# RWKV-7 recurrence and a hard-swish feed-forward on one core: parametric Relus in the weight conversion, and four edits of order

## The chip, the core and the metric

The kernel runs on one core of one Trainium2 chip. Its time is the device time of one execution in microseconds (us), and less is better. Of the kernel before there are three timed runs; beside them one execution was taken by the hardware profiler. The engines are called as in the profile: PE is TensorE's matmul and PEld its weight load, DVE is VectorE, ACT is ScalarE, POOL is GpSimd, SP is SyncE, which here only issues DMAs. L312 is line 312 of the kernel before.

## What is computed

The inputs r, k, v, w, a, b are float32 of 4 batches x 8 heads x 768 positions x 40 features. For each batch and head a 40x40 state runs along the positions:

```python
y[t]  = r[t] @ state
Sa    = state @ a[t]
state = state * w[t] - outer(Sa, b[t]) + outer(v[t], k[t])
```

The outputs y, 3072 tokens of 8 x 40 = 320 features, go through a feed-forward block:

```python
h = x @ w_in                    # 320 -> 2048
g = h * clip(h + 3, 0, 6) / 6
out = g @ w_out                 # 2048 -> 320
```

The two weights come as float64. The kernel sees each element as two 32-bit words (raw[..., 0] the low one, raw[..., 1], called hi, the high one with the sign, 11 bits of exponent and 20 of mantissa) and makes float32 of them itself.

## The kernel before

**The recurrence** is computed in blocks of 64 positions (BL). A unit i is one such block of two batches with all 8 heads; there are 24 units, and four of them (NU) make a group. `prepare(i)` holds the stages that need no state: W (turn w on PE, copy it into wm by L480 and L481 on ACT, one scan on DVE, L484), gam (reciprocal L495, small copies on POOL, the fetch of V), A, B and K (turn the input, multiply by the scan's products; rgam L510, at L513, bt L521, kt L603), factor (rgt on ACT, KBt L590 on POOL), F, E (scores and their mask, L467), EV. `invert` (L643) inverts the lower triangles of a whole group: `fb` and `x` are made first, then 60 dependent small DVE operations (L660 and L666), then two transposes (tb, tt). `third_block` (L685) completes each inverse by two matmul steps, with copies to zs and tinv on ACT; for the first group (`first`) it copies in two halves (`parts`, L689), and POOL copies the diagonal blocks (L710, L711). `step(i)` holds what needs the state: RT, VT, R, S, U (copy L814), UT, C, rS, sn, H, y, and move, which brings the result into xt.

**The feed-forward stream** is a generator whose pieces are put between the other work by `pieces(n)`. A job is one unit and one half of the 2048 features: `expand` issues 32 wide matmuls and a narrow part (`short`: the third 64 rows of the features), whose end leads to L989 (Relu of h + 3 on ACT) and L990 (min and product on DVE); `contract` issues the second matmul (L1015), one job later. While `spread[0]` is set, `short` is not issued at the end of `expand` but later, at the latest after the sixth matmul of the next `contract` (LATEST). h has two PSUM banks, which one job fills. The last jobs are drained by L1334 and L1335.

**The weights** are read in 20 pieces of 128 partitions x 512 elements (`load_weights`, L255). Each call of `next(weights)` takes one step of the conversion:

- L299 (DVE, shift and mask, exponent) and L301 (ACT, Relu with the bias `low`),
- L307 (DVE, low word to the mantissa of the piece before),
- L312 (DVE, product, the piece before is done; a new piece may be loaded),
- L320 (DVE, sign to the exponent),
- L325 (DVE, mantissa bits) and L328 (ACT, to a number in [1, 2)).

So there are five steps to a piece. They are handed out by counters: `fill` and MIXED in the first group's preparation, every third turn of the loop at L1133 while the first inversion runs, and 1.5 or 3 of them for each matmul stage of PLAN (L1161), the written-out order of the first group's `step` stages. In `run` the steps come between a stage's matmuls and the copies of its results. The first feed-forward jobs need 10 pieces, the others all 20.

**Order.** Every engine executes its own instructions in the order of the program, and that order is written out by hand. `by_twos` (L1093) prepares the first and the second group: at t = 0 the stage W of units 0 and 1, at t = 1 gam of both, then A; at t = 3 the stages W of units 2 and 3 and then B of units 0 and 1. All loads go through SP's queue but those of W for unit 1 and one of R, which ACT issues. After the second group `a_block`, `together` and `feed` put the remaining units in between the feed-forward pieces.

Of the kernel before, what the change touches and what calls it, by code (L numbers as in the profile page):

```python
# [8 lines left out]
F32 = mybir.dt.float32  # L9
I32 = mybir.dt.int32  # L10
# [8 lines left out]
HB = BL // 2  # L19
L = 32  # L20
SLOT = 64


def _ap(ap, extra, dims):
# [5 lines left out]
def kernel(  # L30
# [113 lines left out]
    nc.vector.memset(three[:], 3.0)  # L144
    warm = const.tile([P, 1], F32, name="warm")
    nc.scalar.activation(out=warm[:], in_=three[:], func=AF.Relu)
    low = const.tile([P, 1], F32, name="low")
    nc.vector.memset(low[:], -896.0 * 2 ** 23)


    AHEAD = NU + 1
# [103 lines left out]
    def load_weights():  # L255

        todo, homes = weight_pieces(), raw_homes()
        loaded, done, issued = deque(), [], [0]
        upcoming = []

        def load():
            if issued[0] == min(PIECES, limit[0]):
                return False
            if not upcoming:
                upcoming.append(next(homes))
            raw, before = upcoming[0]  # L270
            if before is not None and before not in done:
                return False
            upcoming.clear()
            issued[0] += 1
            out, loads = next(todo)
            for to, src in loads(raw):
                nc.sync.dma_start(out=to, in_=src)
            loaded.append((out, raw))
            return True

        while load():
            pass
        refill.append(load)
        phase[0] = 0
        yield
        before = None
        parts = [grp.tile([P, HD + WPAD], F32, name=f"parts{n}", tag="KBt", bufs=NU + 2)
                 for n in range(2)]
        parts = [t[:, 0:2 * WC].bitcast(U32).rearrange("p (n c) -> p n c", n=2) for t in parts]
        for n in range(PIECES + 1):  # L290
            now = None
            if n < PIECES:
                while load():
                    pass
                out, raw = loaded.popleft()
                hi = raw[:, :, :, 1]
                x = parts[n % 2]
                now = out, raw, x
                nc.vector.tensor_scalar(x, hi, 20, 0x7FF, ALU.logical_shift_right,  # L299
                                        ALU.bitwise_and)  # L300
                nc.scalar.activation(out=x, in_=x, func=AF.Relu, bias=low[:], scale=2.0 ** 23)  # L301
                phase[0] = 1
                yield
            if before:
                out, raw, y = before
                m, yf = raw[:, :, :, 1].bitcast(F32), y.bitcast(F32)
                nc.vector.scalar_tensor_tensor(m, raw[:, :, :, 0], 2.0 ** -52, m, ALU.mult, ALU.add)  # L307
                phase[0] = 2
                yield
                if len(out.shape) == 4:  # L310
                    m, yf = (z.rearrange("p n (j c) -> p n j c", c=out.shape[3]) for z in (m, yf))
                nc.vector.tensor_tensor(out=out, in0=m, in1=yf, op=ALU.mult)  # L312
                converted[0] += 1
                done.append(n - 1)
                while load():
                    pass
                phase[0] = 3
                yield
            if now:
                nc.vector.scalar_tensor_tensor(x, hi, 0x80000000, x, ALU.bitwise_and,  # L320
                                               ALU.bitwise_or)
                phase[0] = 4
                yield

                nc.vector.tensor_scalar(hi, hi, 0xFFFFF, 0x4B000000, ALU.bitwise_and,  # L325
                                        ALU.bitwise_or)
                m = hi.bitcast(F32)
                nc.scalar.activation(out=m, in_=m, func=AF.Copy, bias=-7.0, scale=2.0 ** -20)  # L328
                phase[0] = 5
                yield  # L330
            before = now

    def weight_pieces():

# [51 lines left out]
    def fetch(name, i, engine=None):  # L386

        if i is None or i >= NK:
            return
        x, crossed = {"W": (w, 0), "A": (a, 0), "B": (b, 0), "K": (k, 0), "R": (r, 1),  # L390
                      "V": (v, 1)}[name]
        if name == "V":
            t = values[i % AHEAD]
        else:
            t = (others if i < 2 * NU and i % 2 and name != "R" else inputs)[name]
        g, p = names[i]
        engine = engine or nc.sync
        for q in range(2):
            y = x[2 * p + q, :, g * BL:(g + 1) * BL, :]
            rows = slice(q * BL, (q + 1) * BL)  # L400
            if crossed:
                for s in range(2):
                    engine.dma_start(out=t[rows, 4 * s:4 * s + 4, 0:D],
                                     in_=y[s::2].rearrange("h t e -> t h e"))
            else:
                engine.dma_start(out=t[rows, :, 0:D], in_=y.rearrange("h t e -> t h e"))
        data[i][name + "N"] = t
# [63 lines left out]
    def prepare(i, F):  # L471
        n, o = i % NU, data[i]
        halves = i >= 2 * NU
        def w_stage():
            wt = turn_pairs(o["WN"])
            yield PE

            wv = wm[:].rearrange("p (r m i) -> p r m i", m=2, i=HB + 1)
            x = wt[:].rearrange("p r (q m i) -> p (r q) m i", q=2, m=2)
            nc.scalar.activation(out=wv[:, :, 0, 1:HB + 1], in_=x[:, :, 0, ::-1], func=AF.Copy)  # L480
            nc.scalar.activation(out=wv[:, :, 1, 1:HB + 1], in_=x[:, :, 1, :], func=AF.Copy)  # L481
            fetch("W", following(i))
            prods = o["prods"] = tmp.tile([P, NB, 2, HB + 1], F32, name="prods", bufs=2)
            nc.vector.tensor_tensor_scan(  # L484
                out=prods[:].rearrange("p r m i -> p (r m i)"), data0=wm[:], data1=start[:],
                initial=0.0, op0=ALU.mult, op1=ALU.add,
            )
# [197 lines left out]
    def third_block(F, tb, tt, n, first=False):  # L685


        zs = tmp.tile([P, 2, H, L], F32, name="zs")
        parts = [slice(0, H // 2), slice(H // 2, H)] if first else [slice(0, H)]  # L689
        zp = ps_pair(H, L)  # L690
        for h in range(H):
            for y in range(2):
# [314 lines left out]
    def contract(i, r, gts):  # L1007
# [13 lines left out]
        if r == 0:  # L1021
            sums[i] = op
            if split:
                part = ffn.tile([P, 3 * P], F32, name="part", tag="xt", bufs=6)[:, 0:DM]
                nc.scalar.activation(out=part, in_=op[:], func=AF.Copy, scale=1.0 / 6.0)
                sums[i] = part
        else:
            ob = ffn.tile([P, DM], F32, name="ob", bufs=OB)
            if split:
                nc.vector.scalar_tensor_tensor(out=ob[:], in0=op[:], scalar=1.0 / 6.0,  # L1030
                                               in1=sums.pop(i), op0=ALU.mult, op1=ALU.add)
            else:
                nc.scalar.activation(out=ob[:], in_=op[:], func=AF.Copy, scale=1.0 / 6.0)
            del ready[i]
            g, p = names[i]
            for q in range(2):
                row = (2 * p + q) * T + g * BL
                nc.sync.dma_start(out=out[row:row + BL, :], in_=ob[half(q)])
        yield True


# [45 lines left out]

    STAGES = 9

    RFETCH, EARLY, MIXED = 8, 5, 1 / 3  # L1090
    TWOS = 14

    def by_twos(first, steps, mixed, rate, fill={}):  # L1093


        chains = [by_stages(first + i, prepared(first + i)) for i in range(NU)]
        for t in range(TWOS):

            order = [0, 1] if t < STAGES else []
            order += [2, 3] if t > 5 else []  # L1100
            if t == 3:
                order = [2, 3, 0, 1]
            for i in order:
                run(chains[i], steps if t > 10 else 0, fill.get(t, 0), mixed)
                pieces(rate / 2)
            if t == 10:
                side.append(invert(group_F[-1], third, first == 0))
            yield
# [2 lines left out]
    ring.clear()  # L1111
    ring.extend([("any", 5)] * 5 + [("h", 2)] * 2)
    for name in "WABK":
        for i, engine in enumerate((nc.sync, nc.scalar if name == "W" else nc.sync)):
            fetch(name, i, engine)
    for t, _ in enumerate(by_twos(0, 4, MIXED, 0, {5: 1, 6: 1, 10: 1})):
        if t == 0:
            next(weights)
        limit[0] = {7: 4, 10: 12}.get(t, limit[0])
# [13 lines left out]
    while not third:  # L1133
        aside(1)
        if not third:
            n += 1
            if n % 3 == 1:
                next(weights, None)
            if converted[0] == 2 and not cleared:
                cleared.append(nc.gpsimd.memset(tinv[:], 0.0))  # L1140
            if n % EARLY == 0 and early:
                run(early.popleft())
    assert not early and cleared
    limit[0] = 13
    while phase[0] in (1, 2, 3):
        next(weights)
    firsts = [third_block(*third[-1], n, True) for n in (0, 2)]
    run(firsts[0])
# [181 lines left out]
    for _ in range(2):  # L1330
        for _ in a_block(m):
            pass
        m += 1
    while jobs or next(stream):  # L1334
        next(stream)  # L1335

# [29 lines left out]
```

## Time and profile before

| | |
|---|---|
| median of 3 runs (lowest, highest) | 831.4 us (829.04, 831.72) |
| the profiled execution | 831.98 us, its span 830.2 us |
| PE busy in the span | 746.4 us |
| DVE busy in the span | 547.4 us |
| ACT busy in the span | 321.7 us |
| POOL busy in the span | 156.1 us |
| mean granted TensorE clock | 0.938 |

The span begins with the first instruction and ends with the last; 1.78 us of the execution lie around it. A line of the timeline gives start, duration, engine, line, operation, output and input, and in brackets how long the engine was idle before it and what ended that. Durations of neighbouring DVE and ACT instructions overlap by some 0.1 us, so that sums of durations are a little above the time taken.

### The profile page before, as it was taken

To read this page: it belongs to the slowest core of one execution; us is meant where nothing else is said; L and a number is where in the kernel's file an instruction comes from. 1 tells how busy PE (TensorE), PEld (TensorE's weight loads), DVE (VectorE), ACT (ScalarE), POOL (GpSimd) and SP (SyncE) were. 2 spreads that over 40 slices of the span, in tenths; PEclk is the share of its full clock that TensorE was granted. 3 is DMA by queue.
4 is the path that set the end of the run, shared out by engine and by line. 5 is a ranking of instruction groups with operands and counts; after the bars stand their busy time and mean duration, and the time that the engine had idled before them with its cause. 6 is when DMAs were issued, how large, how long until landed. Compare 5 with 4: busy or idle time off the path is not lost.

```text
span 830.2 us, 35843 instructions
## 1 busy us (share of the span) xinstructions
PE 746.4 (90%) x15832; PEld 632.0 (76%) x15832; DVE 547.4 (66%) x1108; ACT 321.7 (39%) x864; POOL 156.1 (19%) x305
## 2 busy tenths in 40 slices
PE   4732877898999999999999999999999999999997
PEld 3622766686887878788888888878888888888875
DVE  7999697988964769844589654799556685232201
ACT  1323744232344533454433635334553334322211
POOL 3231301122112230321220222112212102000000
PEclk7755587999999999999999999999999999999999
DMA  7573344331133230322331332232232101100000
GB/s 141 85 187 85 91 113 100 70 62 25 21 59 65 52 66 19 59 46 48 56 51 28 60 62 44 42 58 36 45 60 48 22 20 29 29 20 16 15 18 16
DMA packets 174218, 45.05 MB, mean 54 GB/s; under 512 B 157424, under 2 KB 172784, under 8 KB 174064
## 3 DMA queue, kind: packets, MB, share of 16 engines
q1 hardware_dynamic: 171920, 42.44, 26.8%
q8 instruction: 125, 2.05, 1.0%
q10 hardware_dynamic: 2144, 0.33, 0.2%
q14 instruction: 29, 0.24, 0.1%
HBM read 34.08 MB, written 3.93 MB: 46 GB/s over the span
## 4 chain that ended last, share of the span: by engine, by line
PE 70%; DVE 12%; issue 9%; ACT 3%; POOL 2%; DMA 1%; SPq 0%; POOLq 0%; DVEq 0%; ACTq 0%
PE h L974 24%; PE o L1015 22%; PE any L458 4%; PE any L889 3%; PE any L420 2%; PE any L430 2%; PE any L865 2%; DVE prod L660 2%; DVE x L666 2%; PE any L770 1%; PE any L809 1%; DVE parts L320 1%; PE any L830 1%; PE any L846 1%; PE any L696 1%
## 5 line engine op out<-in xcount | busy, mean ns | idle before, releaser
L974 PE MATMUL h<-xt,win 128*128 128x128 f32 (+1 forms) x2304 | 252.8, 284 | 7.0 <-DVE gt L990 7.0
L974 PEld LDWEIGHTS h<-xt,win 128*128 128x128 f32 (+1 forms) x2304 | 232.5, 193 | 25.8 <-issue 8.8
L1015 PE MATMUL o<-wout,gt 128*128 128x320 f32 x768 | 232.8, 445 | 0.2 <-DVE gt L990 0.2
L1015 PEld LDWEIGHTS o<-wout,gt 128*128 128x128 f32 x768 | 139.0, 191 | 51.2 <-issue 1.4
L989 ACT ACTIVATE gt<-h,three 128x512 f32<-128x512 f32 x96 | 62.1, 686 | 104.6 <-PE h L974 104.4
L990 DVE SCALAR_TENSOR_TENSOR gt<-gt,h 128x512 f32<-128x512 f32 x96 | 61.5, 677 | 61.2 <-ACT gt L989 61.2
L660 DVE TENSOR_TENSOR prod<-x 128x30 f32<-128x30 f32 (+9 forms) x180 | 62.8, 349 | 13.5 <-POOL x L651 8.1
L904 POOL TENSOR_TENSOR yg<-ys,gam 128x512 f32<-128x512 f32 x22 | 39.1, 1778 | 167.9 <-DVE ys L902 121.9
L874 DVE TENSOR_TENSOR state<-any,state 40x160 f32<-40x160 f32 (+1 forms) x88 | 27.9, 321 | 62.7 <-PE any L865 36.3
L666 DVE TENSOR_TENSOR x<-x,prod 128x30 f32<-128x30 f32 (+9 forms) x180 | 65.2, 362 | 5.4
L590 POOL TENSOR_TENSOR KBt<-K,rgt 128x320 f32<-128x320 f32 x24 | 21.1, 880 | 248.1 <-ACT rgt L580 217.3
L467 DVE COPY_PREDICATED score<-mask,any 128x256 f32<-128x256 int32 x143 | 53.4, 436 | 4.0 <-PE any L458 3.6
L495 DVE RECIPROCAL gam<-prods 128x256 f32<-128x256 f32 x24 | 41.5, 1741 | 13.5 <-POOL yg L904 13.2
L510 DVE RECIPROCAL rgam<-prods 128x256 f32<-128x256 f32 x24 | 41.8, 1741 | 0.0
L484 DVE TENSOR_TENSOR_SCAN prods<-wm,start 128x528 f32<-128x528 f32 x24 | 30.1, 1254 | 16.6 <-ACT wm L481 14.9
L623 ACT ACTIVATE EV<-any 64x160 f32<-64x160 f32 x92 | 24.8, 295 | 39.8 <-PE any L617 30.3
L902 DVE TENSOR_TENSOR ys<-any,ys 128x256 f32<-128x256 f32 x44 | 16.6, 418 | 34.1 <-PE any L617 18.3
L749 ACT ACTIVATE RT<-any 128x256 f32<-128x256 f32 (+1 forms) x44 | 15.5, 400 | 49.6 <-PE any L430 49.5
L889 PE MATMUL any<-score,KBt 64*64 64x64 f32 x1536 | 31.2, 232 | 2.4 <-DVE score L467 1.6
L889 PEld LDWEIGHTS any<-score,KBt 64*64 64x64 f32 x1536 | 27.5, 144 | 5.3 <-DVE score L467 1.7
L729 ACT ACTIVATE tinv<-any 32x256 f32<-32x256 f32 (+1 forms) x56 | 19.3, 344 | 28.9 <-PE any L719 28.1
L775 DVE TENSOR_TENSOR RR<-any,EV 128x160 f32<-128x160 f32 x44 | 12.2, 318 | 25.6 <-PE any L458 25.4
(193 smaller groups left out, 1077.4 us busy)
## 6 DMA issues: line engine op xcount, KB each, us to landing
B<-in_b_dram SPq DMA_DIRECT2D x48, 80.0 KB
K<-in_k_dram SPq DMA_DIRECT2D x48, 80.0 KB
V<-in_v_dram SPq DMA_DIRECT2D x96, 40.0 KB
out_dram<-ob SPq DMA_DIRECT2D x48, 80.0 KB
R<-in_r_dram SPq DMA_DIRECT2D x92, 40.0 KB
W<-in_w_dram SPq DMA_DIRECT2D x40, 80.0 KB
A<-in_a_dram SPq DMA_DIRECT2D x40, 80.0 KB
xt<-yg SPq DMA_DIRECT2D x72, 40.0 KB
```

What stands on the lines that cost most here:

```text
L458: nc.tensor.matmul(out=o[i][half(q), n, :], lhsT=lhs[half(i, D), n ^ (2 * q * swap), half(q)], rhs=rhs[half(i, D), n, half(q)], start=True ...
L467: nc.vector.copy_predicated(out=x[:, 4 * i:4 * i + 4, :], mask=mask4, data=o[i])
L495: nc.vector.reciprocal(gv[:, :, 0:HB], o["prods"][:, :, 0, 1:HB + 1][:, :, ::-1])
L510: nc.vector.reciprocal(rv[:, :, HB:BL], o["prods"][:, :, 1, 1:HB + 1])
L660: nc.vector.tensor_tensor(out=pv, in0=_ap(x[:], (i + 1) * L + i, [[L, n], [0, i]]), in1=_ap(x[:], i * L, [[0, n], [1, i]]), op=ALU.mult,)
L666: nc.vector.tensor_tensor(out=rest, in0=rest, in1=pv, op=ALU.add)
L889: nc.tensor.matmul(out=y[q][half(s), pr, :], lhsT=o[name][half(q), h * D:h * D + SLOT], rhs=m[name][half(q), 4 * rs + 2 * s + j, :], start ...
L904: nc.gpsimd.tensor_tensor(out=yg[:], in0=m["ys"][:].rearrange("p r q t -> p r (q t)"), in1=o["G"][:], op=ALU.mult)
L974: nc.tensor.matmul(out=hp[c][:, i, :], lhsT=lhsT, rhs=rhs, start=(begun[c] == 0), stop=(begun[c] == 3 * NQ - 1))
L989: nc.scalar.activation(out=gt[:], in_=hp[c][:], func=AF.Relu, bias=three[:], scale=1.0)
L990: nc.vector.scalar_tensor_tensor(out=gt[:], in0=gt[:], scalar=6.0, in1=hp[c][:], op0=ALU.min, op1=ALU.mult)
L1015: nc.tensor.matmul(out=op[:], lhsT=gts[c][:, n, :], rhs=wout[:, c * HJ + r * NQ + n, :], start=((split or r == 0) and c == 0 and n == 0), ...
```

## The change

Six edits are made together.

1. **Conversion.** The sign stays with the exponent: one DVE operation keeps hi's upper 12 bits, two ACT operations (Prelu, a Relu with a slope on the other side) turn them into a signed power of two; the mantissa is taken as an integer with its leading bit set, and the low word is added to it. There are four DVE operations and two ACT operations to a piece, in four steps: L299's place with both Prelus; the product of the piece before; the mantissa bits; the low word. L320 and L328 are gone.
2. **Handing out.** MIXED goes from 1/3 to 0.27; the `fill` of t = 5, 6 and 10 in the first group is dropped. `while phase[0] in (1, 2, 3)` becomes `while phase[0] == 1`.
3. **First scans.** For the first two units of both groups that `by_twos` prepares, W and gam follow each other unit by unit at t = 0; at t = 3 the order is W of unit 2, B of unit 0, W of unit 3, B of unit 1. Unit 0's second copy to wm goes to DVE. The first two W loads are issued half by SP and half by ACT, each.
4. **First third blocks.** ACT and POOL copy whole, no longer in two halves.
5. **Last jobs.** `spread[0]` is cleared before the last jobs are drained.
6. **Last output.** Its second half is issued by ACT.

```diff
+EXP = 916
...
-    low = const.tile([P, 1], F32, name="low")
-    nc.vector.memset(low[:], -896.0 * 2 ** 23)
+    low = const.tile([P, 2], F32, name="low")
+    for i, x in enumerate((EXP - 1792.0, -1792.0 * 2 ** 23)):
+        nc.vector.memset(low[:, i:i + 1], x)
...
-                nc.vector.tensor_scalar(x, hi, 20, 0x7FF, ALU.logical_shift_right,
-                                        ALU.bitwise_and)
-                nc.scalar.activation(out=x, in_=x, func=AF.Relu, bias=low[:], scale=2.0 ** 23)
+                nc.vector.tensor_scalar(x, hi, 0xFFF00000, None, ALU.bitwise_and)
+                nc.scalar.activation(out=x.bitcast(F32), in_=x.bitcast(I32), func=AF.Prelu, bias=low[:, 0:1],
+                                     scale=-2.0 ** -20, alpha=2.0 ** -40)
+                nc.scalar.activation(out=x.bitcast(I32), in_=x.bitcast(F32), func=AF.Prelu, bias=low[:, 1:2],
+                                     scale=-2.0 ** 63, alpha=2.0 ** -40)
...
-                nc.vector.scalar_tensor_tensor(m, raw[:, :, :, 0], 2.0 ** -52, m, ALU.mult, ALU.add)
-                phase[0] = 2
-                yield
...
-                nc.vector.tensor_tensor(out=out, in0=m, in1=yf, op=ALU.mult)
+                nc.vector.tensor_tensor(out=to, in0=m, in1=yf, op=ALU.mult)
...
-                nc.vector.scalar_tensor_tensor(x, hi, 0x80000000, x, ALU.bitwise_and,
-                                               ALU.bitwise_or)
-                phase[0] = 4
-                yield
-
-                nc.vector.tensor_scalar(hi, hi, 0xFFFFF, 0x4B000000, ALU.bitwise_and,
-                                        ALU.bitwise_or)
-                m = hi.bitcast(F32)
-                nc.scalar.activation(out=m, in_=m, func=AF.Copy, bias=-7.0, scale=2.0 ** -20)
-                phase[0] = 5
+                nc.vector.tensor_scalar(hi, hi, 0xFFFFF, 0x100000, ALU.bitwise_and, ALU.bitwise_or)
+                phase[0] = 3
                 yield
+                m = hi.bitcast(F32)
+                nc.vector.scalar_tensor_tensor(m, raw[:, :, :, 0], 2.0 ** -32, hi, ALU.mult, ALU.add)
+                before = out, m, x.bitcast(F32)
+                phase[0] = 4
+                yield
...
+            engine = engines[q] if isinstance(engines, tuple) else engines
...
+            if i == 0:
+                nc.vector.tensor_copy(wv[:, :, 1, 1:HB + 1], x[:, :, 1, :])
+            else:
+                nc.scalar.activation(out=wv[:, :, 1, 1:HB + 1], in_=x[:, :, 1, :], func=AF.Copy)
...
-        parts = [slice(0, H // 2), slice(H // 2, H)] if first else [slice(0, H)]
+        parts = [slice(0, H)]
...
-                nc.sync.dma_start(out=out[row:row + BL, :], in_=ob[half(q)])
+                queue = nc.scalar if q and i == NK - 1 else nc.sync
+                queue.dma_start(out=out[row:row + BL, :], in_=ob[half(q)])
...
-    RFETCH, EARLY, MIXED = 8, 5, 1 / 3
+    RFETCH, EARLY, MIXED = 8, 5, 0.27
...
+            if t < 2:
+                order = [0, 0, 1, 1][4 * t:]
             if t == 3:
-                order = [2, 3, 0, 1]
+                order = [2, 0, 3, 1]
...
-    for t, _ in enumerate(by_twos(0, 4, MIXED, 0, {5: 1, 6: 1, 10: 1})):
+    for t, _ in enumerate(by_twos(0, 4, MIXED, 0)):
...
-    while phase[0] in (1, 2, 3):
+    while phase[0] == 1:
...
+    spread[0] = False
     while jobs or next(stream):
```

More of the change, by code (lines that the diff above doesn't have):

```diff
@@ L304, in load_weights @@
             if before:
-                out, raw, y = before
-                m, yf = raw[:, :, :, 1].bitcast(F32), y.bitcast(F32)
-                nc.vector.scalar_tensor_tensor(m, raw[:, :, :, 0], 2.0 ** -52, m, ALU.mult, ALU.add)
-                phase[0] = 2
-                yield
-                if len(out.shape) == 4:
-                    m, yf = (z.rearrange("p n (j c) -> p n j c", c=out.shape[3]) for z in (m, yf))
-                nc.vector.tensor_tensor(out=out, in0=m, in1=yf, op=ALU.mult)
+                to, m, yf = before
+                if len(to.shape) == 4:
+                    m, yf = (z.rearrange("p n (j c) -> p n j c", c=to.shape[3]) for z in (m, yf))
+                nc.vector.tensor_tensor(out=to, in0=m, in1=yf, op=ALU.mult)
                 converted[0] += 1
@@ L316, in load_weights @@
                     pass
+                phase[0] = 2
+                yield
+            before = None
+            if now:
+                nc.vector.tensor_scalar(hi, hi, 0xFFFFF, 0x100000, ALU.bitwise_and, ALU.bitwise_or)
                 phase[0] = 3
                 yield
-            if now:
-                nc.vector.scalar_tensor_tensor(x, hi, 0x80000000, x, ALU.bitwise_and,
-                                               ALU.bitwise_or)
+                m = hi.bitcast(F32)
+                nc.vector.scalar_tensor_tensor(m, raw[:, :, :, 0], 2.0 ** -32, hi, ALU.mult, ALU.add)
+                before = out, m, x.bitcast(F32)
                 phase[0] = 4
                 yield
-                nc.vector.tensor_scalar(hi, hi, 0xFFFFF, 0x4B000000, ALU.bitwise_and,
-                                        ALU.bitwise_or)
-                m = hi.bitcast(F32)
-                nc.scalar.activation(out=m, in_=m, func=AF.Copy, bias=-7.0, scale=2.0 ** -20)
-                phase[0] = 5
-                yield
-            before = now
     def weight_pieces():
@@ L396, in fetch @@
         g, p = names[i]
-        engine = engine or nc.sync
+        engines = engine or nc.sync
         for q in range(2):
+            engine = engines[q] if isinstance(engines, tuple) else engines
             y = x[2 * p + q, :, g * BL:(g + 1) * BL, :]
@@ L480, in w_stage @@
             nc.scalar.activation(out=wv[:, :, 0, 1:HB + 1], in_=x[:, :, 0, ::-1], func=AF.Copy)
-            nc.scalar.activation(out=wv[:, :, 1, 1:HB + 1], in_=x[:, :, 1, :], func=AF.Copy)
+            if i == 0:
+                nc.vector.tensor_copy(wv[:, :, 1, 1:HB + 1], x[:, :, 1, :])
+            else:
+                nc.scalar.activation(out=wv[:, :, 1, 1:HB + 1], in_=x[:, :, 1, :], func=AF.Copy)
             fetch("W", following(i))
@@ L1113 @@
     for name in "WABK":
-        for i, engine in enumerate((nc.sync, nc.scalar if name == "W" else nc.sync)):
-            fetch(name, i, engine)
-    for t, _ in enumerate(by_twos(0, 4, MIXED, 0, {5: 1, 6: 1, 10: 1})):
+        for i in range(2):
+            fetch(name, i, (nc.sync, nc.scalar) if name == "W" else None)
+    for t, _ in enumerate(by_twos(0, 4, MIXED, 0)):
         if t == 0:
@@ L1138 @@
                 next(weights, None)
-            if converted[0] == 2 and not cleared:
+            if converted[0] >= 2 and not cleared:
                 cleared.append(nc.gpsimd.memset(tinv[:], 0.0))
```

## The prediction

> **What bounds the kernel now.** I read first the busy shares and the forty slices of 20.8 us.
>
> ```profile
> PE 746.4 (90%) x15832; PEld 632.0 (76%) x15832; DVE 547.4 (66%) x1108; ACT 321.7 (39%) x864; POOL 156.1 (19%) x305
> ...
> PE   4732877898999999999999999999999999999997
> ...
> DVE  7999697988964769844589654799556685232201
> ...
> PEclk7755587999999999999999999999999999999999
> ```
>
> From slice 9 PE is full at full clock: the 670 us behind about 160 us are PE's, in an order that the change leaves as it is until the last jobs. Time can be won ahead of that, where DVE has its nines and PE its holes and a clock of 0.5 to 0.8, and at the end. All feed-forward work is still emitted at the same places, so a us won in the front moves everything behind it.
>
> Then the timeline of DVE in the first group's preparation, and in PLAN.
>
> ```profile
> 23.32 0.42 DVE L299 TENSOR_SCALAR parts<-tinv 128x512 uint32<-128x512 uint32 x1
> 24.52 0.69 DVE L320 SCALAR_TENSOR_TENSOR parts<-tinv,parts 128x512 uint32<-128x512 uint32 x1 [0.79 <-ACT parts L301]
> 25.25 0.97 DVE L325 TENSOR_SCALAR tinv<-tinv 128x512 uint32<-128x512 uint32 x1
> 26.14 1.14 DVE L299 TENSOR_SCALAR parts<-tinv 128x512 uint32<-128x512 uint32 x1
> 27.20 3.35 DVE L495 RECIPROCAL gam<-prods 128x256 f32<-128x256 f32 x2
> ```
>
> ```profile
> 108.64 0.69 DVE L320 SCALAR_TENSOR_TENSOR parts<-wout,parts 128x512 uint32<-128x512 uint32 x1
> 109.36 0.43 DVE L325 TENSOR_SCALAR wout<-wout 128x512 uint32<-128x512 uint32 x1
> 109.70 0.42 DVE L299 TENSOR_SCALAR parts<-wout 128x512 uint32<-128x512 uint32 x1
> 110.52 0.69 DVE L307 SCALAR_TENSOR_TENSOR wout<-wout 128x512 f32<-128x512 uint32 x1 [0.39 <-ACT wout L328]
> 111.25 0.69 DVE L312 TENSOR_TENSOR win<-wout,parts 128x512 f32<-128x512 f32 x1
> 111.86 0.69 DVE L320 SCALAR_TENSOR_TENSOR parts<-wout,parts 128x512 uint32<-128x512 uint32 x1
> ```
>
> A piece costs DVE 3.22 us here (108.64 to 111.86), with a wait for ACT's L328. PE's timeline shows who pays: its operations stand behind copies and products that are queued behind conversion steps.
>
> ```profile
> 127.24 1.98 PE L974 MATMUL h<-xt,win 128*128 128x128 f32 x8 [2.99 <-DVE gt L990]
> ...
> 135.51 1.13 PE L458 MATMUL any<-RT,VT 40*64 40x64 f32 x30 [3.25 <-ACT U L814]
> ```
>
> The chain of waits agrees: from 101 to 127 us some 18 us of it are L299 to L328.
>
> **What the Trainium skill says.** "ScalarE: Activation LUTs", section "Same chain, other wiring", puts throughput at one element a cycle whatever the function; L301 (717 ns, with a bias pointer) and L328 (676 ns, immediates) agree, so I price a Prelu at 0.72. Its section "Table sets: the hidden batching unit" says that cheap functions are in every set; no run here shows Prelu, and L146's table load shows 1.28 us. "VectorE: DVE Perf Modes", section "The perf-mode tier table (the rule you actually need)", gives tensor_scalar double rate in float32 and tensor_tensor single; L299 at 0.42 against L312 at 0.69 agree.
>
> **The change part by part.** Counted start to start, the short DVE form takes 0.34 and the long one 0.60.
>
> *Conversion.* Before 2 x 0.34 + 3 x 0.60 = 2.48 a piece, after 2 x 0.34 + 2 x 0.60 = 1.88. ACT has 1.39 before, 1.44 after. Every new DVE step has its Prelu results a whole piece later, so the 0.4 wait goes too. Handing out: I counted steps. Before 14 fall into the first preparation, 13 into the inversion loop, 1 into the first third block, 72 into PLAN (100 in all, over in its 13th line). After 6, 13, 1 and 60 (80 in all, over in the 11th line).
>
> *First preparation.* From 23.32 to 27.20 DVE does conversion only: -3.9 us to gam. Ahead of it, W one half each queue and the second wm copy on DVE (0.35, from at L513's 0.62 for twice the size) start the scans 0.3 to 0.7 earlier, and unit by unit fills idle 0.79 and 0.84 us before scans. But this moves V's loads too, by SP's queue:
>
> ```profile
> 11.90 1.27 SPq L406 DMA_DIRECT2D WA<-in_w_dram  x2
> 13.22 2.02 SPq L277 DMA_DIRECT2D tinv<-in_moe_w_in_dram  x4
> 15.28 6.08 SPq L403 DMA_DIRECT2D V<-in_v_dram  x8
> ...
> 16.25 1.09 PE L420 MATMUL h<-ident,WA 128*128 128x128 f32 x4 [0.77 <-DMA WA<-in_w_dram]
> ```
>
> Unit 3's W now stands behind unit 0's four V loads (4 x 0.68 = 2.7 us): landed about 18.5 in place of 16.2. PE waits for it in order, behind it B of unit 1 and K; scan 3 starts about 20.2 against 19.76, and what was won ahead is lost here. So kt ends at 23.3 as before and gam starts 4 earlier. At 38.53 two steps (1.3 us) go, covered but for 0.5, as fb waits for F on ACT (39.25). B and K of units 2 and 3 are issued behind POOL's KBt, which comes only 1 to 2 us earlier; their landing takes back about 1. Taken: -3.5 at the inversion's start; bounds -1.5 and -5.5.
>
> *Inversion.* DVE is its bound. From 43.6 to 77.7 us it holds 20 steps (9.9 us; those of the preparation's last stages, emitted behind fb, are among them), after the change 19 (8.8): -1.1.
>
> *First third blocks.* Eight copies take 2.31 us, four of 32x256 take 1.55 (rows of later groups). In the first block this is half lost, since the halves let PE begin (U at 84.95, before tinv's end), and a Prelu pair (1.4 us) stands ahead of tinv behind only 1 us of PE work: -0.4. In the second PE waits 0.7 for zs and 1.2 for tinv: -1.0. Bounds together 0 and -3. POOL's copies stay beside ACT's.
>
> *PLAN.* From 101 to 157 us DVE does 12 pieces at 2.48 plus about 4 us of waits for ACT, 34 us; after some 49 steps, 12.25 x 1.88 = 23. Up to -11. PE's waits there sum to 13 (1.3, 2.0, 1.1, 3.0, 3.3, 0.9, 1.6), which is the same size, and say that DVE's time is on the path. Against it: gam of the second group moves ahead of unit 3's sn and H, 3.3 us of DVE (L495) ahead of L874 and L467, for which PE's y waits; it fills 0.86 of idle and lies where 12 steps are gone. Next late are PE's own stages and the second group's inputs. Taken: -8.5; bounds -3 and -16 (PE back at full clock).
>
> *End.*
>
> ```profile
> 811.10 1.29 DVE L990 SCALAR_TENSOR_TENSOR gt<-gt,h 128x512 f32<-128x512 f32 x2 [8.37 <-ACT gt L989]
> 811.84 3.65 PEld L974 LDWEIGHTS h<-xt,win 128*128 128x128 f32 x32 [0.73 <-DVE gt L990]
> ```
>
> Three times (802.18, 811.84, 821.50) PE stands about 0.45 us for gt: the narrow part came after six of eight matmuls. Right behind expand it has a whole contract as cover: -1.3. The last two issues are 0.55 apart; side by side -0.5. Together -1.8, bounds -1 and -2.3.
>
> Sum: -3.5 - 1.1 - 1.4 - 8.5 - 1.8 = -16.3. Span 830.2 - 16.3 = 813.9, with the 1.8 around it 815.7 against 831.98; the median of before is 0.6 lower, so 815.1. I say 815.
>
> **The rivals.** *Inputs and stages take over* (0.17): W of unit 3, B and K land no earlier, and in PLAN copies and inputs replace the steps. Then preparation gives 1.5, PLAN 3, inversion 1.1, blocks 0.4, end 1.5: 7.5, time 824. For it SP issues without a pause from 0.8 to 26 us; against it PLAN's waits name ACT and DVE. *The clock comes back* (0.13): without the 3 us holes PE runs at full clock in PLAN, where about 20 us were at half: PLAN gives 16 and the rest 8: 807. *Tables* (0.07), slower: Prelu is not in the set of Relu and Copy. Each piece then reloads twice, 2.56 us on ACT; for PLAN's 15 pieces that is 38 us, on the queue that carries U, UT and RT. It decides above 0.85 loads a piece on the path (16.3 / (15 x 1.28)); with both, 831 - 16 + 38 = 853. *Nothing* (0.05): the steps left DVE, but PE needs the time anyway: within 0.3% of 831.
>
> **How the numbers follow.** My case has 0.58 and its own range is 809 to 821. I give 806 to 825: with it nearly all of the first rival and half of the second, leaving under 2 in 10. 0.3%, 2.5 us, is about what a measurement can tell here. Faster 0.88, same 0.05, slower 0.07.
>
> **What would show it.** Right: no L320 or L328; Prelus near 0.72 and one table load; gam of units 2 and 3 near 23.3, scan 3 near 20 behind a wait for W; tb near 73; the last product near 130 to 135 in place of 156.5; no PE wait for gt in the last jobs. Wrong: gam before 21 or after 25, waits of conversion for its loads, PE waits of over 10 us from 90 to 140, more table loads.

## The result, and the profile after

| | before | after |
|---|---|---|
| median (lowest to highest) of 4 runs each, us | 831.56 (829.04 to 834.17) | 822.58 (820.46 to 825.33) |
| profiled execution, time / span, us | 831.98 / 830.2 | 823.12 / 821.4 |
| mean granted clock of TensorE | 0.938 | 0.948 |

The ratio of the times is 0.9889 (95%: 0.9868 to 0.9910). The change wins 9 us where 16.3 were forecast; 822.6 lies in the range given (806 to 825), but outside the range of the likeliest case (809 to 821), between its 815 and the first rival's 824 and nearer to the latter.

The page after, busy shares and slices (now 20.5 us each):

```profile
PE 742.0 (90%) x15832; PEld 630.1 (77%) x15832; DVE 534.1 (65%) x1090; ACT 321.5 (39%) x847; POOL 152.4 (19%) x297
...
PE   4723976989999989999999999999999999999998
...
PEclk9855589998999999999999999999999999999999
```

Behind its dip PE's row comes to 9 one slice earlier (the eighth digit, before the ninth; one 8 follows in both). The half clock (fives) lies in slices 3 to 5 as before; the digits in front of it and slices 6 and 7 are higher. A conversion piece in PLAN, on DVE's timeline:

```profile
106.65 0.42 DVE L301 TENSOR_SCALAR parts<-wout 128x512 uint32<-128x512 uint32 x1
106.98 0.69 DVE L312 TENSOR_TENSOR win<-wout,parts 128x512 f32<-128x512 f32 x1
107.58 0.42 DVE L321 TENSOR_SCALAR wout<-wout 128x512 uint32<-128x512 uint32 x1
108.04 0.69 DVE L325 SCALAR_TENSOR_TENSOR wout<-wout 128x512 f32<-128x512 uint32 x1
108.65 0.42 DVE L301 TENSOR_SCALAR parts<-raw_x 128x512 uint32<-128x512 uint32 x1
```

From L301 to the next L301 it takes 2.00 us (3.22 before; 1.88 was counted). In the whole trace no DVE step of the conversion waits for ACT (over 0.15 us); there were ten such waits before. A Prelu takes 0.72 us on ACT (L302, L304), the whole trace has one table load (1.28 us, L147), and the last product of the conversion stands at 135.3 us in place of 156.5.

To place the 9 us I read the same operation in both traces at each border of a stage: the transpose that opens the inversion (fb), the one that closes it (tb), and the fifth and the 89th of the 96 products that end a feed-forward bank (gt).

| stage, us of the traces | before | after | difference | forecast |
|---|---|---|---|---|
| start to fb | 39.85 | 38.74 | -1.1 | -3.5 |
| fb to tb (inversion) | 37.90 | 36.71 | -1.2 | -1.1 |
| tb to fifth gt (third blocks, PLAN) | 90.34 | 83.20 | -7.1 | -9.9 |
| fifth to 89th gt | 619.21 | 621.56 | +2.3 | 0 |
| 89th gt to the end | 42.94 | 41.16 | -1.8 | -1.8 |
| span | 830.24 | 821.37 | -8.9 | -16.3 |

Three rows are off: the first preparation by 2.4, third blocks and PLAN by 2.8, the steady stretch by 2.3. They add up to the miss. The rows are of one trace each, and such a row is not exact to a us: *tail_only* below, whose code is that of before up to the fifth gt, has 38.48 and 87.95 us in the second and third.

### The profile page after: what moved, and what is told of

The parts are those of the page before. It is cut to its first block, busy times and chain, and to the rows that moved or that the text cites. A ratio compares the mean times of both kernels' runs of the same rounds, so it can differ in the third digit from the quotient of the medians.

```text
span 821.4 us, 35781 instructions
## 1 busy us (share of the span) xinstructions
PE 742.0 (90%) x15832; PEld 630.1 (77%) x15832; DVE 534.1 (65%) x1090; ACT 321.5 (39%) x847; POOL 152.4 (19%) x297
## 4 chain that ended last, share of the span: by engine, by line
PE 72%; DVE 9%; issue 9%; SPq 3%; DMA 3%; POOL 2%; ACT 2%; DVEq 0%; POOLq 0%; ACTq 0%
PE h L975 24%; PE o L1016 22%; PE any L456 4%; PE any L890 3%; PE any L418 3%; PE any L428 2%; PE any L866 2%; PE any L810 2%; DVE x L667 1%; SPq L401 1%; PE any L771 1%; DVE prod L661 1%; PE any L831 1%; SPq L404 1%; PE any L697 1%
## 5 line engine op out<-in xcount | busy, mean ns | idle before, releaser
L591 POOL TENSOR_TENSOR KBt<-K,rgt 128x320 f32<-128x320 f32 x24 | 21.2, 884 | 246.9 <-ACT rgt L581 225.5
L496 DVE RECIPROCAL gam<-prods 128x256 f32<-128x256 f32 x24 | 41.8, 1748 | 13.6 <-POOL yg L905 13.2
L730 ACT ACTIVATE tinv<-any 32x256 f32<-32x256 f32 x48 | 18.0, 375 | 30.3 <-PE any L720 29.7
L776 DVE TENSOR_TENSOR RR<-any,EV 128x160 f32<-128x160 f32 x44 | 12.1, 318 | 25.9 <-PE any L456 25.8
```

What stands on the lines that cost most here:

```text
L496: nc.vector.reciprocal(gv[:, :, 0:HB], o["prods"][:, :, 0, 1:HB + 1][:, :, ::-1])
```

## The experiments

### One part alone

*conv_only* is the kernel before with edits 1 and 2 (conversion and handing out), *tail_only* with edits 5 and 6 (the end), *old_scans* is after without edit 3; its main lines, against after:

```diff
-            if t < 2:
-                order = [0, 0, 1, 1][4 * t:]
             if t == 3:
-                order = [2, 0, 3, 1]
+                order = [2, 3, 0, 1]
```

(with W's first loads on one queue each, and unit 0's second copy on ACT again).

> The kernel before with the new conversion and its handing out alone (edits 1 and 2). Theory A (conversion is most of the gain; the edits of the scans give nothing, because unit 3's W lands late): 9.0 less 1.8 for the end and 1.2 for the third blocks, so 825.5 (ratio 0.9928), and the first inversion's first product near 41 to 42. Theory B (the scans gave 1.5 to 2 and the conversion less): 827.5 or more, first product after 43.

> The kernel before with the last jobs' narrow part issued at once and the last output's second half on ACT's queue alone (edits 5 and 6). Both theories: no wait of PE for gt in the last three jobs, 1.8 us less, 829.7. If the clock windows decide instead, the end moves by less than 1 or more than 3.

> The changed kernel without edit 3 (scans, order at t = 3, W's queues and the wm copy as before). Theory A (unit 3's W behind V's loads takes back what the scans win, and PE's F and E stages follow it): same time within 1.5 us, 821 to 823.5; unit 3's W turned near 16.3 in place of 18.3, the stage E of unit 1 over near 28.5 in place of 30, first product near 41. Theory B (the reordering wins its idle 0.8 + 0.8 + 0.7 us): 824.5 to 825, first product near 44.

Measured: conv_only 826.76 us (822.91 to 829.99), ratio 0.9932 (0.9907 to 0.9958); tail_only 829.91, ratio 0.9976 (0.9967 to 0.9986); old_scans 822.55, ratio 0.9888 (0.9869 to 0.9907). The end is worth 2.0 us (0.24% of 832.0), as reckoned. The scans' new order is worth nothing that the times show: with and without it the medians and their intervals are the same, and 1 to 2 us could hide in them. Theory A's time came, and so did its early W of unit 3 (15.64) and E of unit 1 (done by 28.2), and yet the first product of the inversion stands at 43.0, not near 41: something behind E holds it. Conversion alone wins 5.3 us, near to theory A's 6.0, though its interval doesn't shut out B. The gain is not where A had it: fb stands at 39.64, only 0.2 earlier, although gam of unit 2 is 3.9 earlier (23.32), and PE waits twice for B of units 2 and 3 (1.23 and 1.27 us). In the trace most of the gain lies behind tb (84.61 to the fifth gt against 87.95 and 90.34). So the question is what holds fb.

### What holds the first preparation

In after, DVE is done early and waits again at once:

```profile
23.08 3.35 DVE L496 RECIPROCAL gam<-prods 128x256 f32<-128x256 f32 x2
...
30.10 0.44 DVE L465 COPY_PREDICATED score<-mask,any 128x256 f32<-128x256 int32 x1 [3.04 <-PE h L456]
```

PE's timeline in the same stretch:

```profile
18.26 1.09 PE L418 MATMUL h<-ident,WA 128*128 128x128 f32 x4 [2.17 <-DMA WA<-in_w_dram]
...
29.14 0.36 PE L456 MATMUL any<-at,kt 40*64 40x64 f32 x1 [3.38 <-issue]
```

SP's queue in after, and in before the line of A of unit 2:

```profile
15.87 2.62 SPq L401 DMA_DIRECT2D V<-in_v_dram  x4
18.53 2.00 SPq L279 DMA_DIRECT2D tinv<-in_moe_w_in_dram  x4
20.63 1.29 SPq L404 DMA_DIRECT2D A<-in_a_dram  x2
```

```profile
21.46 1.27 SPq L406 DMA_DIRECT2D A<-in_a_dram  x2
```

The wait for unit 3's W is there, 2.17 us, as forecast. Two more suspects stand behind it: a pause of 3.38 us amid PE's products at 29.14 that names no releaser, and SP, which issues almost without a pause up to 23 us, so that A of unit 2 is issued only at 20.63 behind eight loads of V and four of weights. It stood behind the same twelve before (21.46). *v_late* issues the eight V loads behind those of the weights, *loads_late* issues the first weights' loads at t = 6, *v_act* is v_late with ACT as the engine that issues V:

v_act's edit; v_late's is the same without `nc.scalar`:

```diff
-            if i <= 2 * NU:
+            if 2 <= i <= 2 * NU:
                 fetch("V", i)
...
         if t == 0:
             next(weights)
+            for i in range(2):
+                fetch("V", i, nc.scalar)
```

and loads_late's:

```diff
-        if t == 0:
+        if t == 6:
             next(weights)
```

> The changed kernel with the first two units' V loads issued behind the first weight loads, as in the kernel before; all else as changed. Theory A (W of unit 3 behind V's loads is what held the first preparation): unit 3's W turned near 16, scan 3 near 18 without a wait, F two us earlier, first product near 40.5, 820.5 to 821.5. Theory B (PE's F and E stages are held by the weight loads' traffic or by something else at a fixed time): E of unit 1 still over near 30, first product near 42, 822.5.

> The changed kernel with the loads of the first two weight pieces (2 us of SP's queue) issued at t = 6 in place of t = 0. Theory A (SP's issues bound the first preparation: B of unit 3 can land no earlier than the queue lets it): A of unit 2 issued 2 us earlier, fb at 36.7 in place of 38.7, 2 us less in all, 820.5. Theory B (PE's instruction supply or DVE sets fb): fb within 0.5 us of 38.7 and no difference in all.

> The changed kernel with the eight V loads of units 0 and 1 issued by ACT, idle at that time, behind unit 1's wm copy, in place of SP. Theory A (SP's issues bound the first preparation): 5.2 us off SP's queue ahead of A of unit 2, no waits of PE for A, B or K of units 2 and 3, fb near 34.5 in place of 38.7 and DVE's stops before bt gone; 3 to 4 us less in all, 819. Theory B: fb at 38 or later, no difference in all.

v_late: 822.3 us, ratio 0.9887 (0.9866 to 0.9907), the same as after. Unit 3's scan is 1.6 us earlier, the second group of reciprocals (rgam of unit 2) 4.7 earlier (26.05 against 30.77), and fb stands at 38.62, where it was. On PE:

```profile
26.49 1.09 PE L418 MATMUL h<-ident,A 128*128 128x128 f32 x4 [2.39 <-DMA A<-in_a_dram]
```

Everything ahead is early, the pause at the same products is 1.43 us, and PE then waits for A (2.39 and 0.36 us), for B (1.50) and K (0.50). My theory A, that W's place was the bound, falls: W is one member of a queue, and whatever is moved up in that queue moves another down.

loads_late: 825.8 us, ratio 0.991 (0.9885 to 0.9936). fb comes at 36.28, 2.5 earlier, near theory A's 36.7. But that doesn't show A's cause, since PE didn't wait for A, B or K in after either. What is shorter is the pause:

```profile
27.13 0.27 PE L456 MATMUL any<-at,kt 40*64 40x64 f32 x1 [1.20 <-issue]
```

It takes 1.20 us in place of 3.38, which is 2.2 of the 2.5. And the loads moved back are late themselves, inside the inversion, on DVE:

```profile
44.09 0.43 DVE L301 TENSOR_SCALAR parts<-tinv 128x512 uint32<-128x512 uint32 x1 [4.05 <-DMA tinv<-in_moe_w_in_dram]
```

The 4.05 us hold DVE's inversion steps behind the conversion; tb stands at 77.44, 2.0 us later than after's.

v_act: **818.67 us** (816.72 to 819.16), ratio 0.9817 (0.9799 to 0.9835), the fastest version of this study that converts in full. SP's queue after 12 us:

```profile
12.67 1.27 SPq L404 DMA_DIRECT2D WA<-in_w_dram  x2
14.07 1.94 SPq L279 DMA_DIRECT2D tinv<-in_moe_w_in_dram  x4
16.37 1.28 SPq L404 DMA_DIRECT2D A<-in_a_dram  x2
```

A's issue is 4.3 us earlier (16.37 against 20.63), fb stands at 35.27 and tb at 72.28: 3.5 and 3.2 us earlier than in after, though PE takes W of unit 2 later by 0.9 us (15.03 against 14.14). The eight issues take 5.9 us on ACT's queue (7.67 to 13.6 us), where ACT has one copy to make before 16.18.

The clean pair is v_late and v_act, which differ only in the engine that issues V. Their pauses are alike (1.43 and 1.64 us); PE's waits for A, B and K fall from 4.8 to 0.3 us, and fb comes 3.4 us earlier. So the place of A, B and K in SP's queue is shown as one bound of the first preparation. The pause is a second one, and in after it ended last: behind 29.14 PE waits for no load there. It takes 2.9 to 3.4 us in the six traces with after's order of first loads (after, warm, prelu_split and the three that leave work out below) and 1.2 to 1.8 in the six with another order and the new conversion. That both bounds put fb at 38.6 to 38.7, one in v_late and the other in after, is chance. v_act has neither.

The Trainium skill, "DMA: Bandwidth & Descriptors", section "Issuing engines are not separate DMA queues", says that issuing from several engines saves only the sequencer's time to issue, usually small. Here that time counts: eight issues of 0.65 us off SP's queue, and from v_late to v_act the median falls by 3.6 us.

### What is left of the conversion

*prelu_split* puts the second Prelu into the next step, *no_conv* leaves only the loads and the product of each piece, *no_prelu* leaves out the two Prelus, *no_dve* the three DVE operations other than the product. The last three thus leave out part of the conversion.

no_dve drops these three lines and lets the first Prelu read hi; no_conv drops the Prelus as well:

```diff
-                nc.vector.tensor_scalar(x, hi, 0xFFF00000, None, ALU.bitwise_and)
...
-                nc.vector.tensor_scalar(hi, hi, 0xFFFFF, 0x100000, ALU.bitwise_and, ALU.bitwise_or)
...
-                nc.vector.scalar_tensor_tensor(m, raw[:, :, :, 0], 2.0 ** -32, hi, ALU.mult, ALU.add)
```

> The changed kernel with the second Prelu of a piece put into the next step, so that the two no longer stand back to back ahead of a stage's copies on ACT. Theory A (the pair, 1.44 us in one step, holds up U, UT and the first gt, and is part of what PLAN gave less): the first gt at 124 or earlier in place of 125.15, 1 us less in all. Theory B (the pair is hidden; DVE and PE decide): first gt within 0.5 us, no difference in all.

> The changed kernel with only the loads and the product of the conversion: both Prelus and three of the four DVE operations are left out, so the weights are not the right ones. It shows what the conversion still costs: 20 pieces x 1.28 us of DVE and 1.44 of ACT are gone. Theory A (DVE still paces inversion and PLAN): 15 us less or more, 806. Theory B (PE's own stages, its clock and the inputs pace PLAN now; only the inversion's 5 pieces count, 6 us): 813 to 816.

> After without the two Prelus of each piece (the converted weights are not right, all else is there). Dropping the Prelus and three of the four DVE steps had won 11.5 us: 4.7 in the inversion, 6.9 from its end to the fifth gt. Theory A (DVE paces what is left): the Prelus lie on ACT beside DVE's work; inversion as after (36.7), PLAN at most 1 us shorter, 822. Theory B (ACT's queue): in PLAN the copies of U, UT, RT and S stand behind the Prelus, so that PLAN gets 3 to 6 us shorter and the time is 818.

> After with the Prelus and the product of each piece, but without its three other DVE steps (the converted weights are not right). Theory A (DVE): nearly all of the 11.5 us, inversion -4.7, PLAN -6, 811.5. Theory B (ACT's queue): inversion -4.7, as DVE is alone there, PLAN only -1 to -3: 815 to 817.

| | time, us | ratio (95%) | fb to tb | tb to fifth gt |
|---|---|---|---|---|
| after | 822.58 | 0.9889 (0.9868 to 0.9910) | 36.71 | 83.20 |
| prelu_split | 823.16 | 0.9878 (0.9858 to 0.9898) | 37.18 | 85.17 |
| no_prelu | 823.51 | 0.9885 (0.9853 to 0.9918) | 37.42 | 81.33 |
| no_dve | 814.18 | 0.9789 (0.9753 to 0.9824) | 32.10 | 79.80 |
| no_conv | 813.19 | 0.9749 (0.9727 to 0.9772) | 32.01 | 76.31 |

Prelus cost nothing that the times can tell (prelu_split and no_prelu stand where after does), so they lie beside other work: theory B in the first case, A in the second. The DVE steps still cost: no_dve wins 1.0% of before, some 8 us, against after; theory B was nearer, with 815 to 817. no_conv lies in its theory B (813 to 816), in which DVE no longer paces PLAN.

By stages no_dve is 4.6 us shorter in the inversion, which DVE bounds, and 3.4 from tb to the fifth gt; no_conv has 6.9 there, no_prelu 1.9 (both traces are the fastest of their four executions, and two traces of the same code differ by 2.4 in this row). The three steps that no_dve drops take 0.34 + 0.34 + 0.60 = 1.28 us, by the prices of the prediction; in the 15 pieces from tb to the fifth gt that is 19 us, and DVE's busy time falls by 21 there (65.1 to 43.9). For it PE's waits from 23 us behind tb, where the third blocks are over, to the fifth gt are 12.1 us, in after 12.0. What is shorter is PE's busy time from tb on, 59.9 us in place of 65.4, with half clock in 24.6 us of the stretch in place of 36.7. So the 3.4 may be the clock's; that the lighter DVE brought the clock is not shown.

What PLAN waits for has no single name. The largest wait of after there, on PE, then on DVE and ACT:

```profile
125.89 2.08 PE L975 MATMUL h<-xt,win 128*128 128x128 f32 x8 [4.30 <-DVE gt L991]
```

```profile
122.12 0.43 DVE L301 TENSOR_SCALAR parts<-raw_fb 128x512 uint32<-128x512 uint32 x1 [0.46 <-DMA raw_fb<-in_moe_w_out_dram]
...
125.15 1.28 DVE L991 SCALAR_TENSOR_TENSOR gt<-gt,h 128x512 f32<-128x512 f32 x2 [2.00 <-ACT gt L990]
```

```profile
122.58 0.72 ACT L302 ACTIVATE parts<-parts,low 128x512 f32<-128x512 int32 x1 [1.61 <-DVE parts L301]
...
124.44 1.26 ACT L990 ACTIVATE gt<-h,three 128x512 f32<-128x512 f32 x2
```

PE waits for gt; gt waits for ACT's Relu, which stands behind two Prelus and a copy of S; the Prelus wait for L301, and that for its load. This first gt comes 49.7 us behind tb in after, 46.0 in no_prelu, 48.2 in no_dve and 40.0 in no_conv: without one of the two it still stands behind the other. The next waits of PE between 100 and 140 us are for ACT's S (1.5), U (1.5) and UT (1.0), and 1.7 us without a releaser.

### The clock

PE is at half clock from 43.9 to 101.9 us in after. *warm* and *v_act_warm* are after and v_act with 40 transposes whose result nobody uses, in PE's idle time before tb:

```diff
                 run(early.popleft())
+                if not early:
+                    fill = bank("o", [P, DM], 1)
+                    for _ in range(40):
+                        nc.tensor.transpose(out=fill[:, 0:P], in_=ident[:], identity=ident[:])
```

> After, with 40 transposes of 128x128 more on PE (their result is used nowhere), put into its idle 10 us before the first inversion ends, so that PE comes warm to the first third blocks. Theory A (clock): PE was at half clock until 101.9 us in the profiled run of after, and work between 77 and 102 us is paced partly by PE; at full clock from about 75 us on, the first product of the feed-forward stands 2 to 4 us earlier: ratio 0.985. Theory B (order): PE between 77 and 102 waits for ACT's and DVE's copies anyway, which don't run faster; the half clock cost only the single operations between two waits, under 1 us, ratio 0.988 as after. If the half clock ends no earlier in the profile, neither is told apart.

> The version with V's first loads on ACT's queue (818.7 us, ratio 0.9817) with the same 40 transposes. Theory A (clock): half clock ended at 84.4 us there, so less is to be had, 1 us: 0.980. Theory B (order): no change, 0.9817; a loss would mean that the transposes stand in the way of PE's work at the inversion's end.

warm 822.92 us, ratio 0.9902 (0.9872 to 0.9931); v_act_warm 819.49, ratio 0.9858 (0.9829 to 0.9888): nothing won in either, perhaps a little lost in the second. The transposes did bring full clock, but from 72.2 to 79.0 us only; PE then idled 3.4 us before the first products with tb and half clock was granted again, from 79.0 to 106.3. So no theory is told apart over the whole stretch; that nothing came of the few operations at full clock fits theory B (tb 75.46, fifth gt 159.24). A filler that ran up to tb was not tried.

## Why the prediction was partly right

**The conversion's count** was right: 1.88 us counted, 2.00 measured; no wait for ACT, one table load. The rival *Tables* is refuted. gam of unit 2 was forecast for 23.3 and stands at 23.08, scan 3 for 20 and at 20.13, behind the wait for W. One reading was too high: the waits of DVE for ACT from 101 us on, taken as about 4 us, sum to 2.5 in the trace of before.

**First preparation: -3.5 forecast, -1.1 measured.** The failed step is "Taken: -3.5 at the inversion's start", with "their landing takes back about 1" in it. gam came 4.1 us earlier (23.08 against 27.20), and 3.0 of it were taken back. I followed DVE and let the inputs take back only what POOL's KBt holds up. But in both kernels A, B and K of units 2 and 3 stand in one queue behind V's eight loads and the weights', as the fence of the prediction shows: A of unit 2 is issued at 21.46 and at 20.63, B at 26.96 and at 26.93. With its inputs in the same place the stage could not get much shorter, as v_late shows (pause 1.43, fb at 38.62); with issues 4 us earlier it did (v_act, 35.27). In after itself the pause of 3.38 us ended last, which the prediction did not have at all. My first rival had the size of this stage (1.5) and the inputs, but not the pause.

**Inversion: -1.1 forecast, -1.2 measured.** Right in cause as well: no_dve drops three of four DVE steps, by the counted prices 8.8 x 1.28 / 1.88 = 6.0 us of DVE there, and wins 4.6, while DVE's busy time falls by 5.1.

**Third blocks and PLAN: -9.9 forecast, -7.1 measured in this pair of traces.** The blocks gave about what was forecast: the second U stands 14.9 us behind tb in after and 14.5 in old_scans, with whole copies, and 15.9 in conv_only, with halves. At the fifth gt little of it is left in old_scans (84.36 against conv_only's 84.61). PLAN is the mis-sized term: 8.5 forecast. The trace of before has 90.34 here and that of tail_only, whose code is the same up to here, 87.95, so conversion alone (84.61) won 3.3 to 5.7. The step that failed is that DVE's 11 us are "the same size" as PE's waits of 13: equal sums are no proof that one causes the other. From 23 us behind tb to the fifth gt PE waits 14.9 us before (14.8 in tail_only), 10.5 in conv_only, 12.0 in after, and 12.1 in no_dve: the first 8 us off DVE's busy time (73.3 to 65.1) took 3 to 4 us of the waits with them, the next 21 none. PE now waits in other places for DVE's gt and state, ACT's copies and itself.

**Steady stretch: 0 forecast, +2.3 in the traces.** "A us won in the front moves everything behind it" holds up to two places, near 187 and 339 us, which cost 1.1 and 1.2. There after's PE ran at half clock for 6.83 and 3.41 us; before had one such window (3.41 us, from 195.6). The first is no chance event: in all fourteen traces PE pauses 3.1 to 3.2 us at the same products in this place, and half clock comes with it. In after and in before:

```profile
184.55 1.37 PE L618 MATMUL any<-V,score 64*64 64x40 f32 x32 [3.19 <-issue]
```

```profile
194.30 0.95 PE L617 MATMUL any<-V,score 64*64 64x40 f32 x32 [3.20 <-issue]
```

```profile
180.40:183.80 3.40, 0.96 (x34) 0.56 (x32) 3.26 (x5) 0.00 (x0) 3.32 (x5) 1.00 0.07 13
183.80:187.20 3.40, 2.65 (x35) 2.21 (x36) 3.16 (x12) 1.09 (x4) 0.00 (x0) 0.50 0.51 86
```

(The last two are of after: length, busy time of PE, PEld, DVE, ACT and POOL, then PE's clock, DMA share and GB/s.) In after and five other traces (v_late, loads_late, v_act and the two with transposes) the clock falls before the pause is over, and half clock lasts 6.83 us; in the other eight it falls behind the pause and lasts 3.41. The profile names no releaser; DVE masks the score that these products read at 184.02, behind the first steps of the second inversion, four of which take 0.8 us each while POOL makes KBt (L591); later ones take 0.3. The second window stands in the same six traces alone, each time 153.6 us behind the start of the first; PE waits 1.3 us just ahead of it, but it does so in the others too, so its cause is open. The stretch takes 621.1 us on average in the six (620.0 to 622.8) and 619.6 in the eight (618.4 to 620.8). Each version has one trace only, so whether its other executions fall the same way is not shown. The Trainium skill, "TensorE: Matmul & The Clock Gate", section "Part 1: The HAM clock gate", describes a free-running window of about 3.4 us and effects that vary from run to run; the traces agree, with half-clock stretches of multiples of 3.41 us.

**End: -1.8 forecast, -1.8 measured.** PE's three waits are gone, and its last product ends 1.5 us earlier against the 89th gt (1.3 forecast); from there to the end it is 3.86 us in place of 4.17, so the issue on ACT gave 0.3 (0.5 forecast). In the last contract PE runs on while ACT makes gt:

```profile
808.63 1.61 PE L1016 MATMUL o<-wout,gt 128*128 128x320 f32 x5
808.73 1.27 ACT L990 ACTIVATE gt<-h,three 128x512 f32<-128x512 f32 x2 [4.17 <-PE h L975]
```

**The rivals.** *Inputs and stages take over* named both places where gain was lost, and its total (7.5) lies nearer to the measured 9 than mine. It deserved more than 0.17, since its evidence stood on the page. *The clock comes back* came in part at most: from 101 us to the fifth gt half clock covers 11 us in after and 23 before, but 18 in old_scans, which has the same median. From tb to the fifth gt PE's idle time is 17.8 us in after and 20.9 before, its busy time 65.4 and 69.5; so of the 7.1 us about 4 stand in PE's busy time, and how much of that the change brought, and how much the place of the windows in this trace, is not shown. In conv_only, with 44 us of half clock from tb to the fifth gt, the busy time is 68.2 and the idle time alone is shorter (16.4). 807 was far off.

## What to carry to other kernels

Before a gain on a compute engine is carried to the end of a stage, list the inputs that the stage still needs, with the place of each in its queue of issues and the time of one issue: a full queue can take back what is won ahead of it, and moving loads to an idle engine's queue can be worth more than a new order of the work (4 us here, where edit 3 showed nothing). Time freed on a busy engine isn't time won: where PE waits in turn for three engines, here a third to a half of it came through at first (3.3 to 5.7 of the 11 counted), and at most a sixth of the rest (3.4 of 21).

## What the runs showed of the hardware beyond that

- One issue of a load takes 0.64 us in SP's queue, about as much in ACT's (the eight of V: 5.2 us on SP, 5.9 with gaps on ACT); one of a weight piece takes 0.4 to 0.6.
- PE pauses amid products with no releaser in the profile: 3.38 us in after (29.14), 1.43 in v_late (23.53) and 1.64 in v_act (24.98) at the same operations, and 3.02 in v_act at 93.23. Packets of PE's instruction queue (16 KB) end 1.2 to 1.6 us before PE goes on in these four places; for the pause at 29.14 the packet starts 0.6 us behind PE's stop, for those at 23.53 and 24.98 about 1 us ahead of it. That they are the cause is inferred, and was not tested. Ahead of the pause at 184.55 the last packet ends at 180.15.
- After idling PE can stay at half clock through dense work. A stretch of after (busy time of PE, PEld, DVE, ACT and POOL, then PE's clock, DMA share and GB/s):

```profile
86.80:90.20 3.40, 3.40 (x152) 3.22 (x151) 3.37 (x9) 2.15 (x5) 1.25 (x3) 0.50 0.31 77
```

PE is busy for all of it, as from 83.4 to 93.7 us, at clock 0.50. The Trainium skill, "TensorE: Matmul & The Clock Gate", section "Part 1: The HAM clock gate", has full clock come back after one busy window of about 3.4 us; here three were not enough. In v_act and old_scans one was, at the same stage of the program:

```profile
81.00:84.30 3.30, 3.30 (x130) 3.30 (x124) 0.64 (x3) 2.79 (x7) 0.41 (x2) 0.50 0.03 7
84.40:87.80 3.40, 3.16 (x171) 2.70 (x172) 3.30 (x8) 2.52 (x7) 0.74 (x2) 1.00 0.49 129
```

(v_act.) Nearly all of these matmuls are small (32 to 64 rows), so their size alone doesn't decide; what does is open.
